# Five expert items of up to 512 tokens in place of eight of up to 256, in a fused attention, expert and SwiGLU kernel

## The chip, the cores and the metric

The kernel runs on one core of one Trainium2 chip. The metric is the device time of one execution in microseconds (us), as the median of three runs. All times of single instructions come from one profiled execution. The engines are named as in the profile: PE (TensorE matmul), PEld (its weight loads), DVE (VectorE), ACT (ScalarE), POOL (GpSimd), SP (SyncE, which here only issues transfers; SPq is its queue).

## The reference

```
# 1. sparse attention: 2 batches, 8 heads, 768 tokens, head size 64; a window of |i-j| < 16 keys
#    and 24 block summaries                                 -> x: 1536 tokens x 512
# 2. experts, one per token (8 of them, 512 -> 1024 -> 512)
logits = x @ w_gate + modality_bias[modality_id]
e_idx = argmax(logits);  gate = softmax(logits)[e_idx]
for e in range(8):
    h = maximum(x[e_idx == e] @ w1[e], 0);  out[e_idx == e] = gate * (h @ w2[e])
# 3. SwiGLU on all tokens (512 -> 1536 -> 512); its weights are float64
g = x @ w_gate2
return (g * sigmoid(g) * (x @ w_val)) @ w_out
```

With the reference's inputs the argmax sends 46 tokens to expert 3, 651 to expert 5 and 839 to expert 6, and none to the other five; of the first 768 tokens 21, 291 and 456.

## The kernel before, in words

Every product of stages 2 and 3 is made in three passes (`mm3`, lines 775 to 778): both operands are split in a high and a low part, and high x high, high x low and low x high are summed in PSUM. The high part is an ACT copy, the low part a subtraction (`split_w`, lines 756 to 763, for weights, on POOL or DVE; `xh`, `xl` for tokens; `hh`, `hl` for the hidden layer, both from PSUM on ACT and DVE).

The stages run one after another on PE: attention (to about 102 us), the items of the experts (to about 302 us), the SwiGLU layer (six slices `fb` of 256 hidden columns by three groups of 512 tokens, 72 matmuls of 512 columns each time).

An **item** is a run of tokens of one expert: a pair (P) is two blocks of 128 tokens, a single (S) one block. `KIND` fixes eight of them, "PPSPPSPP". Item 0 is chosen when the first 768 tokens are routed and runs while the others are; items beyond the eight run in a loop at the end, `For_i(0, n_over)`. For an item POOL gathers the tokens (`xs`, an indirect transfer for each block, line 723), DVE multiplies them by their gate (`scale_x`, line 730), PE turns them (line 740), and then four chunks of the first matrix (`hidden`) and four of the second (`project`) follow. In a pair the weights stand in the array and 256 tokens move: 24 matmuls of 256 columns a chunk, 192 an item. In a single the tokens stand and the weights move: 48 matmuls of 256 columns and 24 of 512.

A chunk is 512 KB of weights. The lists of chunks are loaded and split ahead of use: four buffers for the loaded chunk (`raw`) and four for its parts (`wc`); `split_to(done + 4)` stands ahead of each chunk's products, and a load is issued by SP when a `raw` buffer is free. `POOLS` gives the low part of every second chunk to POOL, the others to DVE.

Routing goes through short DVE operations and small matmuls: `route` (ranks), `route_where`, `route_items(i0, i1)` (a mask `bo` on DVE, line 517, then 24 small matmuls `bo` by `a`, line 523, which give the row numbers `idx` of those items). The program is written out in the order of each engine's queue: an engine that waits holds back all that stands behind it.

The float64 weights of the SwiGLU layer arrive as 64-bit words and are decoded by five DVE operations each (`decode`, lines 1145 to 1167), then split by ACT and POOL. Those of slice 0 are decoded during the last two items, a step behind each chunk (`bg_step`).

Of the kernel before, what the change touches and what calls it, by code (L numbers as in the profile page):

```python
# [19 lines left out]
def sparse_attention_moe_swiglu_kernel(  # L20
# [28 lines left out]
    # queries go in groups of 64; a group sees 96 keys, from 16 before it on, and the summaries of all blocks  # L49
# [20 lines left out]
    NP, NSG = KIND[1:].count("P"), KIND[1:].count("S")  # L70
    MAXP = (NTOK + E * (IT // 2 - 1)) // IT
    NI = 1 + MAXP + E
    NIC = NI * 2
# [20 lines left out]
    b_p = [None, attn.enter_context(tc.tile_pool(name="b1", bufs=1))]  # L94
# [86 lines left out]
    # the mask of the window and the bias of the summaries as a product: ml.T @ mr  # L181
# [16 lines left out]
    # keys: per group of queries the window and the summaries; queries: the two heads of a pair on the diagonal  # L198
# [19 lines left out]
    # the averages over blocks of 32 tokens of a chunk of v, in the rows of the summaries  # L218
# [31 lines left out]
    cs = [const.tile([128, 2, 2 * E], F32, name=f"cs{i}") for i in range(4)]  # L250
# [18 lines left out]
    mtab = const.tile([128, NI, 2, E], F32, name="mtab")  # L269
# [7 lines left out]
    def route_consts():  # L277
# [75 lines left out]
    a1 = {}  # L353

    def route(g, a, b):
# [52 lines left out]
        a0 = w_p.tile([128, 8, 128], BF16, tag="a0", bufs=1, name="a0")[:, 0:n]  # L408
# [12 lines left out]
    def route_early():  # L421
        # the first item: up to 256 tokens of the expert that has the most in the first group
        b = GROUPS[0][1]
        c0 = cnt[:, 0]
        w = w_p.tile([128, 6, E], F32, tag="r_ew", bufs=1, name="r_ew")
# [4 lines left out]
        nc.vector.tensor_scalar(out=n0, in0=m8, scalar1=-1.0, scalar2=float(-IT), op0=ALU.mult, op1=ALU.max)  # L430
        nc.vector.tensor_scalar(out=sc[0][:, 16:17], in0=m8, scalar1=float(IT), scalar2=None, op0=ALU.min)
# [3 lines left out]
        nc.vector.scalar_tensor_tensor(out=w[:, 2, 0:2], in0=fs.to_broadcast([128, 2]), scalar=-16.0, in1=kc[:, 0],  # L435
                                       op0=ALU.mult, op1=ALU.add)
# [3 lines left out]
        TB = [128, b, 2]  # L440
        nc.vector.tensor_tensor(out=bo[:, 0:b, 0:2], in0=w[:, 2, 0:2].unsqueeze(1).to_broadcast(TB),
# [14 lines left out]
        load_to(4)  # L456
# [6 lines left out]
    def route_where():  # L463
        # where the items lie: per expert the pairs and singles before it
# [16 lines left out]
        u = w_p.tile([128, 2, E], F32, tag="r_u", bufs=1, name="r_u")  # L481
        u_r.append(u)
        nc.vector.scalar_tensor_tensor(out=u[:, 1], in0=cs[0][:, 0, E:2 * E], scalar=2.0, in1=wm16, op0=ALU.mult,
                                       op1=ALU.add)
        nc.vector.scalar_tensor_tensor(out=u[:, 0], in0=cs[3][:, 0, E - 1:2 * E - 1], scalar=-2.0, in1=wm16,
                                       op0=ALU.mult, op1=ALU.add)

    def route_items(i0, i1):
        todo = [(gg, a, t) for gg, (a, b) in enumerate(GROUPS) for t in range(b - a)]
        n = i1 - i0  # L490
        IE9 = [128, n, 2, E + 1]
        IE = [128, n, 2, E]
# [9 lines left out]
        mu = w_p.tile(IE, F32, tag=f"r_mu{i0}", bufs=1, name="r_mu")  # L502
        nc.vector.tensor_tensor(out=mu, in0=mtab[:, sl], in1=u_r[0].unsqueeze(1).to_broadcast(IE), op=ALU.mult)
        mu2 = w_p.tile(IE, F32, tag=f"r_mv{i0}", bufs=1, name="r_mv")
# [8 lines left out]
        sl_c = w_p.tile([128, n, 2], F32, tag=f"r_sc{i0}", bufs=1, name="r_sc")  # L513
        nc.vector.tensor_tensor(out=sl_c, in0=kc[:, sl], in1=sm.unsqueeze(2).to_broadcast([128, n, 2]), op=ALU.add)
# [6 lines left out]
        for i, (gg, a, t) in enumerate(todo):  # L521
            for j in range(2):
                nc.tensor.matmul(out=ip[:, 0:2 * n], lhsT=a1[gg, j][:, t, :], rhs=bo[:, a + t, ss],
                                 start=(i == 0 and j == 0), stop=(i == NT - 1 and j == 1))
        nc.vector.tensor_copy(out=idx[:, ss], in_=ip[:, 0:2 * n])
        yield

    def route_starts():
        # first column of each item: the tokens of the items before it
        IE = [128, NI - 1, 2, E]  # L530
# [183 lines left out]
    def open_moe():  # L714
        for nm, n in (("xg", 1), ("h", NC1), ("raw", 4), ("wc", 4)):
            pl[nm] = moe.enter_context(tc.tile_pool(name=nm, bufs=n, side="right", reuse_waits="tile"))
# [649 lines left out]
```

## Time and profile before

| | |
|---|---|
| median of three runs | 616.27 us (615.70 to 616.77) |
| span of the profiled execution, first to last instruction | 614.8 us |
| PE busy | 573.1 us, 93% |
| DVE, ACT, POOL busy | 397.1, 233.4, 197.1 us |
| mean granted clock of TensorE | 0.971 of full speed |

The profiled execution has no other time of its own than its span; the median of the runs is 1.5 us above it. The span is counted from the first instruction to the last. A busy share is an average over stages that have different limits.

### The profile page before, as it was taken

The numbers are of one execution on the slowest core, as the hardware profiler recorded it, in microseconds if no ns is written. First come the engines' busy times: TensorE is split into PE (matmuls) and PEld (weight loads), VectorE is DVE, ScalarE is ACT, GpSimd is POOL, SyncE is SP. The second block draws the span as 40 slices with busy tenths as digits, with TensorE's granted clock in tenths as the row PEclk, the third lists the DMA queues.
The fourth block names the chain that finished last, engine by engine and source line by source line (L and its number), as shares of the span: only waits on it lengthen the run. The fifth ranks groups of instructions, "written<-read, shape, count | busy, mean of one in ns | idle before, by whom it ended". The sixth has DMA issues, their size and how long they took to land.

```text
span 614.8 us, 9915 instructions
## 1 busy us (share of the span) xinstructions
PE 573.1 (93%) x3840; PEld 499.3 (81%) x3840; DVE 397.1 (65%) x616; ACT 233.4 (38%) x375; POOL 197.1 (32%) x222
## 2 busy tenths in 40 slices
PE   6989999779999998977699999999999999999995
PEld 6879988779989997976678888888888888888884
DVE  5577787679987449999116836827835946773332
ACT  5767946425565556454213332211211221221110
POOL 5682013343674556745101211301110310220025
PEclk8979999988999999999899999999999999999998
DMA  9999239463779768662121322402212220200013
GB/s 246 211 224 227 78 88 278 125 209 118 242 261 320 220 223 261 206 206 69 60 81 32 107 69 68 138 0 69 74 63 64 74 68 1 68 1 1 1 68 138
DMA packets 76322, 77.69 MB, mean 126 GB/s; under 512 B 25252, under 2 KB 57008, under 8 KB 76080
## 3 DMA queue, kind: packets, MB, share of 16 engines
q1 hardware_dynamic: 74192, 70.19, 39.7%
q0 software_dynamic: 2080, 6.82, 3.2%
q8 instruction: 32, 0.52, 0.4%
q14 instruction: 18, 0.15, 0.1%
HBM read 70.46 MB, written 6.35 MB: 125 GB/s over the span
## 4 chain that ended last, share of the span: by engine, by line
PE 48%; issue 1%; POOL 1%; POOLq 0%; DVE 0%
PE ps_T L776 11%; PE ps_T L778 11%; PE ps_T L777 11%; PE ps_S L777 3%; PE ps_S L776 3%; PE ps_S L778 3%; PE ps_P L776 1%; PE ps_P L778 1%; PE ps_P L777 1%; PE ps_V L778 1%; PE ps_V L777 1%; PE ps_V L776 1%; POOL out_dram L1313 0%; POOLq L1361 0%; DVE acc L1308 0%
## 5 line engine op out<-in xcount | busy, mean ns | idle before, releaser
L762 POOL TENSOR_TENSOR wl<-da,wh 128x1024 fp32r<-128x1024 f32 x18 | 45.8, 2544 | 228.3 <-ACT wh L761 223.8
L776 PE MATMUL ps_T<-yh,wh 128*128 128x512 f32 x288 | 114.3, 397 | 4.8 <-issue 4.8
L778 PE MATMUL ps_T<-yh,wl 128*128 128x512 f32 x288 | 113.8, 395 | 0.0
L777 PE MATMUL ps_T<-yl,wh 128*128 128x512 f32 x288 | 113.2, 393 | 0.0
L762 POOL TENSOR_TENSOR wl<-raw,wh 128x1024 fp32r<-128x1024 f32 x32 | 82.4, 2577 | 56.8 <-ACT wh L761 55.6
L1291 DVE TENSOR_TENSOR hv<-sg,ps_T 128x512 f32<-128x512 f32 x36 | 24.7, 685 | 95.9 <-PE ps_T L778 95.2
L761 ACT ACTIVATE wh<-raw 128x1024 fp32r<-128x1024 f32 x64 | 67.0, 1056 | 24.1 <-DMA raw<-in_moe_w_dram 14.8
L762 DVE TENSOR_TENSOR wl<-raw,wh 128x1024 fp32r<-128x1024 f32 x32 | 59.0, 1843 | 20.3 <-ACT wh L761 19.9
L776 PEld LDWEIGHTS ps_T<-yh,wh 128*128 128x128 f32 x288 | 54.4, 189 | 17.1 <-issue 5.0
L778 PEld LDWEIGHTS ps_T<-yh,wl 128*128 128x128 f32 x288 | 54.3, 188 | 13.1
L777 PEld LDWEIGHTS ps_T<-yl,wh 128*128 128x128 f32 x288 | 54.5, 189 | 12.7
L1293 ACT ACTIVATE fh<-hv 128x512 fp32r<-128x512 f32 x36 | 22.8, 633 | 110.1 <-DVE hv L1291 110.1
L1289 ACT ACTIVATE sg<-ps_T 128x512 f32<-128x512 f32 x36 | 21.5, 596 | 97.0 <-PE ps_T L778 97.0
L778 PE MATMUL ps_S<-hh,wl 128*128 128x256 f32 x184 | 53.7, 292 | 4.0 <-DVE wl L762 4.0
L777 PE MATMUL ps_T<-xl,wh 128*128 128x256 f32 x192 | 53.9, 281 | 2.7 <-DVE xl L743 2.7
L776 PE MATMUL ps_T<-xh,wh 128*128 128x256 f32 x192 | 54.5, 284 | 0.0
L776 PE MATMUL ps_S<-hh,wh 128*128 128x256 f32 x184 | 54.0, 294 | 0.2 <-DVE ex_r L391 0.2
L777 PE MATMUL ps_S<-hl,wh 128*128 128x256 f32 x184 | 53.4, 290 | 0.4 <-DVE hl L791 0.4
L778 PE MATMUL ps_T<-xh,wl 128*128 128x256 f32 x192 | 53.8, 280 | 0.0
L1295 DVE TENSOR_TENSOR fl<-hv,fh 128x512 fp32r<-128x512 f32 x36 | 25.4, 705 | 25.2 <-ACT fh L1293 25.2
L778 PEld LDWEIGHTS ps_S<-hh,wl 128*128 128x128 f32 x184 | 36.6, 199 | 4.4 <-DVE wl L762 4.4
L777 PEld LDWEIGHTS ps_T<-xl,wh 128*128 128x128 f32 x192 | 36.3, 189 | 3.2 <-DVE xl L743 3.1
(273 smaller groups left out, 1227.4 us busy)
## 6 DMA issues: line engine op xcount, KB each, us to landing
raw<-in_moe_w_dram SPq DMA_DIRECT2D x64, 512.0 KB, 4.0
r<-in_moe_w_gate_dram SPq DMA_DIRECT2D x6, 1024.0 KB, 5.1
r<-in_moe_w_val_dram SPq DMA_DIRECT2D x6, 1024.0 KB, 5.1
r<-in_moe_w_out_dram SPq DMA_DIRECT2D x6, 1024.0 KB, 5.0
ve<-in_v_dram SPq DMA_DIRECT2D x20, 192.0 KB, 5.3
ld<-in_k_dram SPq DMA_DIRECT2D x12, 256.0 KB, 6.0
ld<-in_q_dram SPq DMA_DIRECT2D x12, 256.0 KB, 5.5
x_d<-x SPq DMA_DIRECT2D x12, 256.0 KB, 3.9
```

Of the source, the lines that this page charges most:

```text
L761: nc.scalar.activation(out=wh, in_=src, func=ACTF.Copy)
L762: eng.tensor_tensor(out=wl, in0=src, in1=wh.bitcast(F32), op=ALU.subtract)
L776: nc.tensor.matmul(out=out_, lhsT=ah, rhs=bh, start=start, stop=False)
L777: nc.tensor.matmul(out=out_, lhsT=ah, rhs=bl, start=False, stop=False)
L778: nc.tensor.matmul(out=out_, lhsT=al, rhs=bh, start=False, stop=stop)
L1289: nc.scalar.activation(out=sg, in_=gp_, func=ACTF.Silu)
L1291: nc.vector.tensor_tensor(out=hv, in0=sg, in1=vp_, op=ALU.mult)
L1293: nc.scalar.activation(out=hh, in_=hv, func=ACTF.Copy)
L1295: nc.vector.tensor_tensor(out=hl, in0=hv, in1=hh.bitcast(F32), op=ALU.subtract)
```

## The change

The items are now T (three blocks, 384 tokens), Q (four, 512), S, Q, P: "TQSQP". The pairs' code serves all kinds but S, with the columns of a matmul equal to the item's tokens; where two halves don't fit in one PSUM bank each takes its own. The counts of Q, P and S come from the bits of each expert's count. The second matrix's chunks are now half of the rows by half of the columns (512 x 256 in place of 256 x 512), so that two chunks finish half of the outputs, which are then stored (`store_y`) while the other half is computed; in S the 24 matmuls of 512 columns become 48 of 256. There are three `raw` and three `wc` buffers, four for gathered blocks. POOL makes the low part of every chunk but the odd ones of item 0 and of S (`DVES`). The float64 weights come, and are decoded, in halves of 512 KB; two steps behind each chunk. In item 0 `route_items(2, NI)` comes with its small matmuls between the second and the third chunk of `project`.

```diff
-    KIND = "PPSPPSPP"
+    KIND = "TQSQP"
+    BLOCKS = {"T": 3, "Q": 4, "P": 2, "S": 1}
...
+    RB, WB = 3, 3
     def open_moe():
-        for nm, n in (("xg", 1), ("h", NC1), ("raw", 4), ("wc", 4)):
+        for nm, n in (("xg", 1), ("raw", RB), ("wc", WB)):
...
-            t = pool.tile([128, DM + 1], F32, tag="xs", bufs=2, name="xs")
+            t = pool.tile([128, DM + 1], F32, tag="xs", bufs=4, name="xs")
...
     def load_w(pool, e, which, c):
-            src = w2[bass.ds(e, 1), 256 * c:256 * c + 256, :]
+            src = w2[bass.ds(e, 1), 512 * (c % 2):512 * (c % 2) + 512, 256 * (c // 2):256 * (c // 2) + 256]
...
+    def project(c, hs, w, yp, cols=(0, 1)):
+        for k in range(4):
+            kk = 4 * (c % 2) + k
+            h = hs[kk // 2]
+            for dd in cols:
...
+                mm3(y, w[0][:, k, sl], w[1][:, k, sl], h[0][:, kk % 2, :], h[1][:, kk % 2, :],
...
-    POOLS = [0] + list(range(3, len(preps), 2))
+    DVES = [i for i, (wn, j, c) in enumerate(preps) if (KIND[j] == "S" or i < 2 * NC1) and i % 2]
...
     hidden_0(3)
-    yp = y_banks()
+    yp = [y_banks(CT, "S")]
     project_0(0, False)
...
     xs = gather(pl["xg"], *idx_of(1))
+    rg.append(route_items(2, NI))
     project_0(1)
-    rg.append(route_items(3, NI))
     adv(6)
     scale_x(xs)
-    project_0(2)
-    project_0(3)
-    x = split_of(1, xs)
     while rg:
         adv(1000)
     attn.close()
...
+    store_y(0, yp[0], slice(0, CT), slice(0, CT))
+    yp.append(y_banks(CT, "T"))
+    project_0(2)
+    x = split_of(1, xs)
+    project_0(3)
+    store_y(1, yp[1], slice(0, CT), slice(0, CT))
     sexc = route_starts()
...
         if j == NS - 2:
-            bg += [decode((wn, 0), fw_p) for wn in "gvo"]
+            bg += [decode(wn, 0, i, fw_p) for wn in "gvo" for i in range(2)]
+            load64()
+            load64()
...
         for c in range(NC1):
-            split_to(done + 4)
+            split_to(done + WB)
...
-            bg_step()
+            bg_step(2)
```

**The order on PE** in the second half of item 0, at the small matmuls of the second `route_items`. Before, they stand behind all four chunks of `project` (the rows with `ps_S`) and the turning of item 1's tokens:

```order
L776 MATMUL ps_S<-hh,wh 128x256
L777 MATMUL ps_S<-hl,wh 128x256
L778 MATMUL ps_S<-hh,wl 128x256
L740 MATMUL ps_V<-ident,xs 128x128 x4
L740 MATMUL ps_P<-ident,xs 128x128 x4
L523 LDWEIGHTS a_1421
L523 MATMUL ps_V<-bo,a_1421 128x30
```

Now they stand behind the second chunk, and chunks three and four come after them:

```order
L802 MATMUL ps_S<-hh,wh 128x384
L803 MATMUL ps_S<-hl,wh 128x384
L804 MATMUL ps_S<-hh,wl 128x384
L540 LDWEIGHTS a_1431
L540 MATMUL ps_V<-bo,a_1431 128x76
L540 LDWEIGHTS a_1432
L540 MATMUL ps_V<-bo,a_1432 128x76
```

They have moved ahead of half of `project`, and have 76 columns in place of 30.

**The order on DVE** at the same place: `idx` of item 1, a weight split (`wl`), and the operations of the second `route_items` up to the mask `bo`. Before:

```order
L525 CAST idx<-ps_V 128x4
L762 TENSOR_TENSOR wl<-raw,wh 128x1024
L497 TENSOR_TENSOR r_lt<-cs_203,kk__208 128x270
L500 TENSOR_TENSOR mtab<-r_lt 128x240
...
L517 TENSOR_TENSOR bo<-r_sc,code 128x12x30
L730 TENSOR_SCALAR xs<-xs 128x512 x2
```

Now:

```order
L542 CAST idx<-ps_V 128x4
L789 TENSOR_TENSOR wl<-raw,wh 128x1024
L514 TENSOR_TENSOR r_lt<-cs_203,kk__208 128x513
L517 TENSOR_TENSOR mtab<-r_lt 128x456
...
L534 TENSOR_TENSOR bo<-r_sc,code 128x12x76
L756 TENSOR_SCALAR xs<-xs 128x512 x4
```

The order is the same, each operation is about twice as wide, and four blocks are scaled in place of two.

**The order on POOL** over the last two items, with the gathers (`xs`), the weight splits and the low parts of the decoded weights (`gl`, `vl`, `ol`). Before, from the gather of the last item on:

```order
L723 DMA xs<-x_d,idx 128x513 x2
L762 TENSOR_TENSOR wl<-raw,wh 128x1024 x3
L762 TENSOR_TENSOR wl<-da,wh 128x1024
L762 TENSOR_TENSOR wl<-raw,wh 128x1024
L1183 TENSOR_LOAD tab
L762 TENSOR_TENSOR wl<-raw,wh 128x1024
L762 TENSOR_TENSOR wl<-da,wh 128x1024
```

Now:

```order
L749 DMA xs<-x_d,idx 128x513 x2
L789 TENSOR_TENSOR wl<-raw,wh 128x1024 x3
L1220 TENSOR_TENSOR gl<-da,gh 128x4x128
L789 TENSOR_TENSOR wl<-raw,wh 128x1024 x2
L1220 TENSOR_TENSOR gl<-da,gh 128x4x128
L789 TENSOR_TENSOR wl<-raw,wh 128x1024 x2
L1220 TENSOR_TENSOR vl<-da,vh 128x4x128
```

The low parts of the decoded weights stand between splits that are now all on POOL.

## Rows read from the trace of the kernel before

**Rows 1.** The page: busy time, share of the span and instructions of each engine.

```profile
PE 573.1 (93%) x3840; PEld 499.3 (81%) x3840; DVE 397.1 (65%) x616; ACT 233.4 (38%) x375; POOL 197.1 (32%) x222
```

**Rows 2.** Busy time by stretch: items 0, 2, 4 to 7, the gap behind, SwiGLU.

```profile
core 0: us, PE busy (x) PEld busy (x) DVE busy (x) ACT busy (x) POOL busy (x), PEclk, DMA share, GB/s
102.38:138.56 36.18, 27.29 (x242) 26.23 (x241) 26.66 (x59) 14.26 (x19) 14.44 (x9) 0.91 0.62 179
...
165.03:180.61 15.58, 14.32 (x114) 12.46 (x113) 14.02 (x23) 11.11 (x16) 11.62 (x5) 1.00 0.80 259
...
204.76:228.01 23.25, 23.25 (x198) 23.25 (x197) 10.21 (x12) 11.99 (x16) 11.40 (x6) 1.00 0.73 240
228.01:243.93 15.92, 13.42 (x90) 11.73 (x89) 13.93 (x17) 11.01 (x16) 10.35 (x6) 1.00 0.89 281
243.93:270.03 26.10, 24.59 (x205) 24.19 (x204) 24.23 (x19) 13.62 (x18) 16.78 (x8) 1.00 0.63 205
270.03:301.83 31.80, 25.11 (x194) 24.10 (x192) 24.41 (x21) 10.90 (x15) 14.10 (x6) 0.95 0.23 70
301.83:306.60 4.77, 0.00 (x1) 0.01 (x1) 0.42 (x1) 1.67 (x2) 0.00 (x0) 0.96 0.42 120
306.60:604.80 298.20, 298.20 (x1285) 242.26 (x1286) 168.85 (x205) 65.08 (x99) 47.47 (x31) 0.99 0.17 57
```

**Rows 3.** What PE waited for, longest in total first.

```profile
PE ps_V L523 <- DVE bo L517: 5.3, 1, 5.3
PE ps_T L776 <- issue: 4.8, 1, 4.8
PE ps_V L740 <- DVE xs L730: 4.4, 2, 3.0
PE ps_S L778 <- DVE wl L762: 4.0, 2, 2.1
PE ps_T L777 <- DVE xl L743: 2.7, 2, 2.3
```

**Rows 4.** Busy time by stretch, inside runs of matmuls of one width.

```profile
125.16:128.51 3.35, 3.35 (x21) 3.35 (x19) 1.71 (x3) 0.00 (x0) 1.06 (x2) 0.50 0.60 187
204.76:216.07 11.31, 11.31 (x99) 11.31 (x97) 5.73 (x7) 6.27 (x9) 5.24 (x3) 1.00 0.85 278
330.84:347.50 16.66, 16.66 (x73) 13.48 (x73) 15.02 (x14) 6.49 (x10) 4.98 (x2) 1.00 0.40 127
```

**Rows 5.** Groups of instructions: count, busy us, mean ns, idle before.

```profile
L762 POOL TENSOR_TENSOR wl<-raw,wh 128x1024 fp32r<-128x1024 f32 x32 | 82.4, 2577 | 56.8 <-ACT wh L761 55.6 <-DVE wl L762 1.1
L761 ACT ACTIVATE wh<-raw 128x1024 fp32r<-128x1024 f32 x64 | 67.0, 1056 | 24.1 <-DMA raw<-in_moe_w_dram 14.8 <-PE ps_S L777 7.0 <-POOL wl L762 1.3
L762 DVE TENSOR_TENSOR wl<-raw,wh 128x1024 fp32r<-128x1024 f32 x32 | 59.0, 1843 | 20.3 <-ACT wh L761 19.9
L723 POOL DMA_INDIRECT xs<-x_d,idx x14 | 17.4, 1242 | 18.3 <-PE ps_P L740 6.6 <-DVE code L453 4.6 <-DVE idx L525 4.5
```

**Rows 6.** Timeline of DVE: start us, duration us.

```profile
209.37 1.23 DVE L762 TENSOR_TENSOR wl<-raw,wh 128x1024 fp32r<-128x1024 f32 x1 [0.26 <-ACT wh L761]
...
248.80 2.85 DVE L1152 TENSOR_SCALAR da<-r 128x1024 int32<-128x1024 int32 x1
...
252.29 3.44 DVE L762 TENSOR_TENSOR wl<-raw,wh 128x1024 fp32r<-128x1024 f32 x1
```

**Rows 7.** Timeline of POOL at the same places.

```profile
248.67 2.42 POOL L762 TENSOR_TENSOR wl<-raw,wh 128x1024 fp32r<-128x1024 f32 x1
251.86 2.79 POOL L762 TENSOR_TENSOR wl<-raw,wh 128x1024 fp32r<-128x1024 f32 x1 [0.77 <-ACT wh L761]
```

**Rows 8.** Timeline of DVE: first and last of nine operations of `route_items`.

```profile
135.19 0.43 DVE L497 TENSOR_TENSOR r_lt<-cs,kk__208 128x270 f32<-128x270 f32 x1
...
137.58 0.53 DVE L517 TENSOR_TENSOR bo<-r_sc,code 128x360 bf16<-128x360 f32 x1
```

**Rows 9.** The 64 loads of expert weights: from issue to landing.

```profile
DMA to landing us min/median/max: 3.2/4.0/8.8
```

**Rows 10.** Timeline of ACT: the high part of a decoded weight, and its wait.

```profile
293.39 1.06 ACT L761 ACTIVATE wh<-da 128x1024 fp32r<-128x1024 f32 x1 [7.95 <-DVE da L1162]
```

More of the change, by code (lines that the diff above doesn't have):

```diff
@@ L66, in sparse_attention_moe_swiglu_kernel @@
     IT = 256
-    KIND = "PPSPPSPP"
+    KIND = "TQSQP"
+    BLOCKS = {"T": 3, "Q": 4, "P": 2, "S": 1}
     NS = len(KIND)
[L70 to L73, printed above, removed]
+    NQ, NP, NSG = (KIND.count(kd) for kd in "QPS")
+    CT = 128 * BLOCKS["T"]
+    MAXQ = 3
+    assert 385 * (MAXQ + 1) > NTOK and NQ <= MAXQ
+    NOQ, NOP = 2 * (MAXQ - NQ), E - NP
+    NI = NS + NOQ + NOP + E - NSG
+    NB = 4
+    NIC = NI * NB
     KD = DM // 128
@@ new lines, in hidden, with low @@
+        for f0 in range(0, 2, per):
+            p = bank("T")[:, 0:per * n].rearrange("p (f c) -> p f c", f=per)
+            for f in range(f0, f0 + per):
+                sl = slice(128 * f, 128 * f + 128)
+                for kk in range(KD):
+                    mm3(p[:, f - f0, :], w[0][:, kk, sl], w[1][:, kk, sl], x[0][:, kk, :], x[1][:, kk, :], kk == 0,
+                        kk == KD - 1)
+            fs = slice(f0, f0 + per)
+            nc.scalar.activation(out=hh[:, fs], in_=p, func=ACTF.Relu)
+            def low(p=p, fs=fs):
+                nc.vector.scalar_tensor_tensor(out=hl[:, fs], in0=p, scalar=0.0, in1=hh[:, fs].bitcast(F32),
+                                               op0=ALU.max, op1=ALU.subtract)
+            if later is None:
+                low()
+            else:
+                later.append(low)
@@ new lines, in y_banks, with store_y @@
+    def y_banks(n, tag):
+        if n == 256:
+            return [bank(tag).rearrange("p (d c) -> p d c", d=2)]
+        return [bank(tag)[:, 0:n].rearrange("p (d c) -> p d c", d=1) for _ in range(2)]
+    def store_y(dp, yp, a, v_):
+        for i, y in enumerate(yp):
+            nd = 2 // len(yp)
+            ds = slice(2 * dp + nd * i, 2 * dp + nd * i + nd)
+            nc.scalar.activation(out=yh[:, ds, a], in_=y, func=ACTF.Copy)
+            nc.vector.tensor_tensor(out=yl[:, ds, v_], in0=y, in1=yh[:, ds, v_].bitcast(F32), op=ALU.subtract)
@@ L1038, in project_0 @@
         if split:
-            split_to(NC1 + c + 4, 2 * NC1 if c == 0 else None)
-        project(c, hs[c], ready.pop(("w2", 0, c)), yp)
+            split_to(NC1 + c + WB, 2 * NC1 if c == 0 else None)
+        project(c, hs, ready.pop(("w2", 0, c)), yp[c // 2])
     hs, later = [], []
@@ L1053, in sparse_attention_moe_swiglu_kernel @@
         adv(1000)
[L1054 removed]
+    rg.append(route_items(1, 2))
     adv(6)
@@ L1163, in decode @@
                                        op1=ALU.bitwise_or)
-        if key[0] == "g":
-            load64("o", key[1])
+        load64()
         yield
-        fw[key] = split_w(pool, a.bitcast(F32), nc.gpsimd, (key[0] + "h", key[0] + "l"))
+        if i == 0:
+            whole = [128, 2, DM] if wn == "o" else [128, KD, 256]
+            fw[wn, fb] = [pool.tile(whole, F32R, tag=wn + x, name=wn + x) for x in "hl"]
+        part = (slice(None), slice(i, i + 1)) if wn == "o" else (slice(None), slice(None), slice(128 * i, 128 * i + 128))
+        wh, wl = (t[part] for t in fw[wn, fb])
+        nc.scalar.activation(out=wh, in_=a.bitcast(F32), func=ACTF.Copy)
+        nc.gpsimd.tensor_tensor(out=wl, in0=a.bitcast(F32), in1=wh.bitcast(F32), op=ALU.subtract)
     def bg_step(n=1):
@@ L1175, in bg_step, with before @@
                 bg.pop(0)
-    store_y(yp, slice(0, IT), slice(0, IT))
+    store_y(0, yp[0], slice(0, CT), slice(0, CT))
[4 more added lines that the diff above has]
+    store_y(1, yp[1], slice(0, CT), slice(0, CT))
     sexc = route_starts()
+    def before(j):
+        return min(NTOK, sum(128 * BLOCKS[kd] for kd in KIND[:j]))
     done = 2 * NC1
```

386 lines of the change are left out of this document (195 added, 191 removed).

## The prediction

> **What bounds the kernel now.** I read the page's busy table first: PE works 93% of the span [rows 1], so only what PE does, or waits for, can change the time. The stretches come next, cut at the items [rows 2]. In SwiGLU PE is busy for 298.20 of 298.20 us; nothing in the change makes its 1296 matmuls fewer, so no gain is to be had there. From the first product of item 0 to the last of item 7 it is 102.38 to 301.83, 199.45 us, and the items differ: item 4, a pair, takes 23.25 us with PE busy throughout, but item 0 takes 36.18 with PE busy for 27.29, item 6 takes 26.10 and item 7 takes 31.80 with 25.11 busy; the singles, 15.58 and 15.92. The chain of waits says for what [rows 3]: in item 0 the mask `bo` (5.3 us) and the scaled tokens (3.0 us of the 4.4), late in the last items `wl` and `xl`, all of them on DVE, which is busy 24.23 of 26.10 and 24.41 of 31.80 us there [rows 2]. A wait costs more than itself: behind the 5.3 us the granted clock is 0.50, the level of 1.2 GHz, for 3.35 us [rows 4], half of which is lost.
>
> DVE is that slow because of POOL. One `wl` takes 1.23 us on DVE alone; at 252.29 it took 3.44, and its end lies 1.08 us behind the end of the POOL split that began at 251.86 for 2.79; the decoding step at 248.80 likewise ends 0.56 us behind POOL's [rows 6, 7]. So one of the two waits for the other, instruction by instruction.
> The page "SBUF — State Buffer" of the Trainium skill, section "SBUF: two separate sides", says the same: a DVE operation of two SBUF inputs, or in a two-port mode, and a GpSimd operation lock a shared port pair for the whole instruction. The trace agrees (3.44 against 1.23 us); if they shared it by halves instead, the S item below would cost some 4 us less.
>
> **The change part by part.**
>
> *Matmuls.* The columns stay 1792 (384+512+128+512+256 against six times 256 and two times 128), but wide matmuls are cheaper by the column: 96 of 256 columns take 11.31 us, 117.8 ns each, and 72 of 512 take 16.66, 231.4 ns [rows 4] (the counts in the rows hold the neighbours still in flight). So a Q saves 192 x (2 x 117.8 - 231.4) = 0.8 us against two pairs; T's 384 columns, which no row shows, lie between the two, 175 ns by the middle. By themselves the wider matmuls give some 2 us. The gain must come from the waits.
>
> *The stages one by one*, against item 4's 23.25 us = 192 x 117.8 ns + 0.6 for four transposes and the like.
>
> T: 192 x 0.175 = 33.5. Routing's small matmuls take about 1.7 (item 0's 27.29 busy, less 22.6 for its pair, less some 3 at half clock); 16 transposes of item 1's tokens 1.5 (at most 0.16 each by item 4's rest, 0.09 taken); 76 columns in place of 30, 0.6. The first mask keeps its place on PE, behind the first chunk of `project`, but each chunk ahead of it lasts 4.2 us rather than 2.8, so it should be ready: 5.3 us gone. In its place comes a **new wait**: the small matmuls of the second `route_items` stand between chunks two and three of `project`, and PE holds for its mask. Nine DVE operations took 135.19 to 138.11, 2.9 us [rows 8]; twice as wide, about 5. They begin behind a `wl` that can't start before chunk one ends (its buffer) and takes ACT 1.06 and DVE 1.23, so 2.3 + 5 = 7.3 us against chunk two's 4.2: 3.1 us late, 3.5 taken; nothing at best, 8 if the lock adds two POOL splits. Behind PE stand chunks three and four and item 1. The same wait again costs 1.5 at half clock. A third gathered block ahead of item 0: at most a further 1.24 [rows 5], 0.9 taken; and 0.8 for `project`'s waits on its weights, since on POOL the split of chunk three stands behind four gathers of 1.24. T: 44.
>
> Q: 192 x 0.2314 = 44.4, with 4 to 8 transposes and stores 0.8, and 0.8 for item 1's first bank, freed behind `route_starts` on DVE: 46.0 each. A chunk lasts 5.6 us, so one load of 4.0 (8.8 at worst [rows 9]), one ACT copy of 1.06 and one POOL split of 2.58 [rows 5] are covered by two chunks in hand. The decoding hides here too: two half steps a chunk, about 0.6 us each and up to 2.4 of waiting for POOL, beside two `hl` of 0.7: 5.2 to 7.4 a chunk at the worst, 3.5 as a rule.
>
> S: 96 x 117.8 ns = 11.3, with 16 transposes 1.5, token matmuls and turns 1.4: 14.2 of work. The buffers hold two chunks ready; the other six need three splits on POOL (2.58) and three on DVE (1.23), one after another: 11.4 us, and the scaling of four blocks (1.7) on the same port. With 1.06 for ACT and as much for its two stores ahead, and 1.4 for the last chunk, 16.7; the ring of three `raw` buffers can't refill faster than (4.0 + 1.06 + 2.58) / 3 = 2.5 a chunk, which adds 2 to 4. I take 20.3; 15.5 at best (the singles' 1.3 us of waiting as now), 26 at landings of 8.8: (8.8 + 3.6) / 3 = 4.15 for six chunks.
>
> P, the last: 22.6 + 0.6, and 1.0 for a late split: POOL makes all eight (20.6 of 22.6 us). No DVE split is left in it, where the last two pairs had eight: that is where 6.69 us of item 7's wait go. 24.2; bounds 23.25 and 31.8.
> The page "GPSIMD Engine Reference", section "Key points", puts DVE at about twice GpSimd's speed for elementwise work, which speaks against this move; 1.23 against 2.58 us agrees, and the decoding rival below is priced by it.
>
> *At nothing:* the gap of 4.77 us behind the items stays. The 24 chunks of 512 KB that are no longer loaded only free the queues. Half-size decoding in SwiGLU gives DVE 15 more short operations a slice; by their widths [rows 8] (0.10 us for 90 more elements, so 0.13 fixed) that is 2 us a slice, on 168.85 busy of 298.20. PE's 49.7 us a slice cover it; without that cover it would be 10 us in five slices.
>
> Sum: T 44 + 2 x 46.0 + 20.3 + 24.2 = 180.5 against 199.45, **-19**; I keep 0.5 for DVE operations I haven't listed: -18.4. The span becomes 596.4, and with the 1.5 us by which the median stands above it, **598 us**.
>
> **The rivals.**
>
> 1. *As summed*, 593 to 603. Chance 0.53.
> 2. *The new waits don't come*: the mask ready in time (T 39.5), S with its present waits (16.5), P clean: 10 less, 588. For it: the DVE chain at 135.19 ran without a split of POOL beside it. Against: DVE is the busier engine in every row where PE waits [rows 2]. 0.15.
> 3. *The lock hits the new order harder*: two POOL splits inside the mask's chain (+4.8, and half clock), S at 26, P at 28: 607 to 612. For it 3.44 against 1.23. 0.20.
> 4. *Slower: decoding holds POOL.* POOL's queue has six low parts of decoded weights between splits that are now all its own, and each stands behind ACT, which waited 7.95 us for DVE's decoding [rows 10]. Half the size, half the wait: 4 us, six times 24: 598 + 24 = 622. It decides from 3.1 us each (18.4 / 6). Against: a Q chunk has 3 us of slack, and DVE has lost 24 of its 32 splits (1.84 each, 44 us). 0.05.
> 5. *The change doesn't do what it says*: an item is left over and runs in the loop. By the inputs' counts T takes 384 of expert 6, which leaves 455 (one Q), 651 (a Q and a P) and 46 (an S): exactly the list. 640 or fewer in place of 651 would leave one over, for at least 22.6 + a load and split of 7.6 + gathers, 36: 634. 0.02.
> 6. *No change that can be told*: rivals 3 and 4 in part. 0.05.
>
> **How the numbers follow.** The likeliest is 598. 588 to 610 takes in rivals 1 to 3 but for their ends, about 0.82. A change within 0.2% (1.2 us) is about what a measurement of this kernel can't tell from none. Faster by more: 0.53 + 0.15 + 0.20 and a little of 6, 0.90; same 0.03; slower 0.07.
>
> **What would show it.** PE's stretches: T 42 to 46 us with one wait of 3 to 5 us for `bo` before the 76-column matmuls, clock 0.50 behind it; each Q 45 to 47 with PE busy all through; S 18 to 23 with waits for `wl` and `hl`; P under 25; SwiGLU 298 again. No ACT wait for `da` above 4 us. DVE busy at most two thirds of each Q. It is wrong if a Q shows waits on `wh` or `wl` (loading or POOL bounds after all), if P passes 28 (rival 4), if the loop runs, or if SwiGLU is no longer full.

## The result and the profile after

The changed kernel took 621.29 us (median of 13 runs, 618.17 to 624.77) against 618.19 for the kernel before (13 runs, 615.70 to 620.59): ratio 1.0065, 95% interval 1.0041 to 1.0090. The forecast was 598 (588 to 610); it was wrong in its sign too. The profiled execution has a span of 622.1 us and took 623.85, above its median, so its stretches sum to more than the 3.1 us between the medians.

The page's busy row of the changed kernel, as [rows 1]:

```profile
PE 575.0 (92%) x3396; PEld 486.2 (78%) x3396; DVE 381.9 (61%) x688; ACT 212.3 (34%) x370; POOL 194.5 (31%) x252
```

PE's stretches in the changed kernel, columns as in [rows 2]: T, Q, S, Q, P, the gap, SwiGLU.

```profile
109.11:163.06 53.95, 44.69 (x283) 43.28 (x281) 31.13 (x72) 17.36 (x29) 17.59 (x11) 0.85 0.32 100
163.06:207.70 44.64, 44.64 (x197) 36.43 (x197) 21.47 (x47) 15.53 (x22) 23.87 (x13) 1.00 0.34 114
207.70:231.55 23.85, 18.69 (x145) 17.17 (x144) 15.71 (x22) 12.45 (x18) 9.31 (x5) 0.86 0.53 173
231.55:278.10 46.55, 45.77 (x207) 37.21 (x205) 28.19 (x33) 18.13 (x26) 29.49 (x15) 1.00 0.54 174
278.10:308.58 30.48, 25.41 (x193) 24.59 (x191) 22.48 (x20) 11.33 (x17) 18.95 (x9) 0.94 0.35 116
308.58:313.98 5.40, 0.00 (x1) 0.01 (x1) 0.43 (x1) 1.67 (x2) 0.00 (x0) 0.95 0.03 6
313.98:612.18 298.20, 298.20 (x1286) 242.22 (x1287) 185.24 (x280) 67.50 (x114) 48.33 (x46) 1.00 0.17 56
```

Both Qs are full, the second but for a wait of 0.78 us for a `wl`, and as long as forecast (91.2 us, 92.0 said), and SwiGLU is the same 298.20 us. The loss lies in the three others. From 102.38, where item 0 began before, T takes 60.7 us, not 44: its first product comes at 109.11, and then it takes 53.95. S takes 23.85, not 20.3, and P 30.48, not 24.2. These are 16.7 + 3.6 + 6.3 = 26.6 us more than forecast.

What PE waited for in the changed kernel (reader, releaser and line: us in total, times, longest), as [rows 3]:

```profile
PE ps_V L540 <- DVE bo L534: 4.6, 1, 4.6
PE ps_S L804 <- POOL wl L789: 4.5, 2, 2.4
PE ps_V L717 <- DMA ve<-ve: 4.3, 2, 4.2
PE ps_T L802 <- DVE hl L822: 3.5, 1, 3.5
PE ps_S L804 <- DVE hl L871: 3.2, 2, 2.1
PE ps_V L768 <- DVE xs L756: 2.6, 1, 2.6
PE ps_P L768 <- DVE xl L771: 2.2, 3, 1.1
```

The wait for `bo` was forecast (3.5). The ones for `hl` (L822) and `xs` lie in T and were not. The wait for `ve` lies in the attention, at 37.7, and comes and goes from execution to execution: in the traces of the changed kernel and of its ten variants below, which don't alter that part, the first transposes of tokens behind the attention began between 98.8 and 102.3 us. The 1.7 us by which they began later here than before (102.34 against 100.64) is therefore not put down to the change.

Three times in T a DVE operation ended with a POOL split that had begun within 0.2 us of it. First DVE, then POOL in the changed kernel's timeline (start us, duration us):

```profile
102.87 2.49 DVE L756 TENSOR_SCALAR xs<-xs 128x512 f32<-128x512 f32 x1 [0.76 <-DMA xs<-x_d,idx]
125.49 2.24 DVE L492 TENSOR_TENSOR cs<-cs 128x24 f32<-128x24 f32 x1
145.09 2.47 DVE L531 TENSOR_TENSOR r_sc<-kc,r_sm 128x76 f32<-128x76 f32 x1
```

```profile
102.75 2.34 POOL L789 TENSOR_TENSOR wl<-raw,wh 128x1024 fp32r<-128x1024 f32 x1 [5.95 <-DMA raw<-in_moe_w_dram]
125.31 2.38 POOL L789 TENSOR_TENSOR wl<-raw,wh 128x1024 fp32r<-128x1024 f32 x1 [0.24 <-ACT wh L788]
145.10 2.35 POOL L789 TENSOR_TENSOR wl<-raw,wh 128x1024 fp32r<-128x1024 f32 x1
```

Elsewhere in these traces they take 0.48, 0.18 and 0.22 us. Each stands on the way to one of PE's waits: `xs` at 105.42, the chain of the first mask ahead of the deferred `hl` at 130.06, the second mask `bo` at 148.75. On DVE the first mask and the deferred `hl` came in this order:

```profile
129.33 0.21 DVE L534 TENSOR_TENSOR bo<-r_sc,code 128x48 bf16<-128x48 f32 x1
129.46 1.01 DVE L822 SCALAR_TENSOR_TENSOR hl<-ps_T,hh 128x384 fp32r<-128x384 f32 x2
```

and on PE the wait for that `hl` came ahead of the products that use the mask:

```profile
130.06 0.69 PE L802 MATMUL ps_T<-xh,wh 128*128 128x384 f32 x1 [3.53 <-DVE hl L822]
139.10 0.76 PE L540 MATMUL ps_V<-bo,a 128*128 128x4 bf16 x24
```

The waits cost twice: right behind the 3.5 us for `hl`, PE works 4.01 us at a granted clock of 0.50, which is 1.2 GHz.

```profile
130.06:134.07 4.01, 4.01 (x13) 4.01 (x13) 2.01 (x3) 0.00 (x0) 0.00 (x0) 0.50 0.41 136
```

In P the last chunk's copy on ACT stands behind a decoded weight's, as in rival 4. Two of the forecast's own signs of being wrong came with it: P past 28 us, and a wait of ACT for `da` above 4 us. ACT's timeline, with the wait in brackets, then POOL's split of the same chunk and PE's wait for it:

```profile
299.88 0.63 ACT L1219 ACTIVATE oh<-da 128x512 fp32r<-128x512 f32 x1 [5.36 <-DVE da L1210]
300.42 1.04 ACT L788 ACTIVATE wh<-raw 128x1024 fp32r<-128x1024 f32 x1
```

```profile
301.85 2.35 POOL L789 TENSOR_TENSOR wl<-raw,wh 128x1024 fp32r<-128x1024 f32 x1
```

```profile
304.25 0.39 PE L804 MATMUL ps_S<-hh,wl 128*128 128x256 f32 x1 [2.08 <-POOL wl L789]
```

So there were two theories. One: a handful of separate waits, each made by the order of a queue (DVE's, ACT's, SP's) and by the lock between DVE and POOL, make the loss, and each can be mended. The rival: the splits, most of them now on POOL, bound the items, so that a wait taken away comes back.

### The profile page after: what moved, and what is told of

Read it like the earlier page. It is cut to its first block, busy times and chain, and to the rows that moved or that the text cites. A ratio compares the mean times of both kernels' runs of the same rounds, so it can differ in the third digit from the quotient of the medians.

```text
span 622.1 us, 9023 instructions
## 1 busy us (share of the span) xinstructions
PE 575.0 (92%) x3396; PEld 486.2 (78%) x3396; DVE 381.9 (61%) x688; ACT 212.3 (34%) x370; POOL 194.5 (31%) x252
## 4 chain that ended last, share of the span: by engine, by line
PE 48%; issue 1%; POOL 1%; POOLq 0%; DVE 0%
PE ps_T L802 11%; PE ps_T L804 11%; PE ps_T L803 11%; PE ps_S L803 3%; PE ps_S L802 3%; PE ps_S L804 3%; PE ps_V L804 1%; PE ps_P L802 1%; PE ps_V L803 1%; PE ps_V L802 1%; PE ps_P L803 1%; PE ps_P L804 1%; POOL out_dram L1381 1%; POOLq L1426 0%; POOL tk L1380 0%
## 5 line engine op out<-in xcount | busy, mean ns | idle before, releaser
L802 PE MATMUL ps_T<-yh,gh 128*128 128x512 f32 x144 | 57.5, 399 | 5.4 <-issue 5.4
L804 PE MATMUL ps_T<-yh,gl 128*128 128x512 f32 x144 | 57.1, 396 | 0.0
L803 PE MATMUL ps_T<-yl,gh 128*128 128x512 f32 x144 | 56.9, 395 | 0.0
L802 PE MATMUL ps_T<-yh,vh 128*128 128x512 f32 x144 | 56.8, 394 | 0.0
L804 PE MATMUL ps_T<-yh,vl 128*128 128x512 f32 x144 | 56.7, 394 | 0.0
L803 PE MATMUL ps_T<-yl,vh 128*128 128x512 f32 x144 | 56.3, 391 | 0.0
L802 PE MATMUL ps_T<-xh,wh 128*128 128x512 f32 (+2 forms) x128 | 47.0, 367 | 3.5 <-DVE hl L822 3.5
L804 PE MATMUL ps_T<-xh,wl 128*128 128x512 f32 (+2 forms) x128 | 46.6, 364 | 1.4 <-POOL wl L789 1.4
L803 PE MATMUL ps_T<-xl,wh 128*128 128x512 f32 (+2 forms) x128 | 46.4, 363 | 0.0
L822 DVE SCALAR_TENSOR_TENSOR hl<-ps_T,hh 128x512 fp32r<-128x512 f32 (+1 forms) x28 | 17.8, 648 | 26.9 <-ACT hh L819 26.9
L1207 DVE SCALAR_TENSOR_TENSOR db<-r,da 128x512 int32<-128x512 int32 x36 | 31.9, 887 | 0.2
```

The costliest lines, as they stand in the source:

```text
L802: nc.tensor.matmul(out=out_, lhsT=ah, rhs=bh, start=start, stop=False)
L803: nc.tensor.matmul(out=out_, lhsT=ah, rhs=bl, start=False, stop=False)
L804: nc.tensor.matmul(out=out_, lhsT=al, rhs=bh, start=False, stop=stop)
L822: nc.vector.scalar_tensor_tensor(out=hl[:, fs], in0=p, scalar=0.0, in1=hh[:, fs].bitcast(F32), op0=ALU.max, op1=ALU.subtract)
L1207: nc.vector.scalar_tensor_tensor(out=b, in0=lo, scalar=29, in1=a, op0=ALU.logical_shift_right, op1=ALU.bitwise_or)
```

## The experiments

No kernel here leaves any of the computation out. Ratios are to the kernel before, run on the same chip beside each; the changed kernel's is 1.0065. The intervals are 0.4 to 0.8% wide, 2 to 5 us. The ratios aren't those of the two medians; by the medians, each less that of the kernel before beside it, the gains named below come out up to 2.7 us smaller (5.1 us for e1_hl_now, 1.7 for e6_dec_q2, 10.0 for e7_all). Only e1_hl_now, e6_dec_q2, e7_all, e9_mend2 and e10_mend_rb4 have intervals that lie apart from the changed kernel's.

**`hl` at once** (e1_hl_now).

```diff
-    hidden_0(2, later)
+    hidden_0(2)
```

> The changed kernel, with the low parts `hl` of the first item's third hidden chunk made at once on DVE, not behind the mask's chain. Theory A (single waits in the first item make the loss): a T chunk now needs two banks, so the fourth hidden chunk waits for those `hl`; PE's wait of 3.5 us at 130.06 goes, and with it about 2.0 us of half clock behind it (4.01 us at 0.50); the mask's chain then starts 1.0 us later and still ends before the first chunk of `project` does. 5.5 us faster than the changed kernel: 616, ratio to the kernel before about 0.997. Rival B (the splits on POOL bound the item, so a wait that is taken away comes back at the next `wl`): the wait appears at `wl` or `bo` in the next 20 us, the stretch 109 to 163 keeps its 54.0 us within 1.5, 620.

Ratio 0.9970 (0.9946 to 0.9994), 615.54 us: 5.9 us from the changed kernel (the difference of the ratios, 0.0095, times 618; so below). The wait is gone, and T's 53.95 us are 46.81:

```profile
106.56:153.37 46.81, 41.08 (x283) 39.95 (x282) 28.90 (x72) 17.41 (x29) 17.61 (x11) 0.93 0.37 115
```

The waits for `bo` (4.6) and `xs` (2.6) stayed as they were. This one deferred operation is more than the whole loss against the kernel before: with it mended, the changed kernel is the faster one, if by little.

**Small matmuls later** (e2_small_behind).

```diff
     adv(6)
     scale_x(xs)
+    yp.append(y_banks(CT, "T"))
+    project_0(2)
     while rg:
         adv(1000)
```

> The changed kernel, with the small matmuls of the second `route_items` behind the third chunk of the first item's `project` in place of ahead of it. Theory A: PE's 4.59 us wait for `bo` and 1.5 to 2 us of half clock go (one chunk of 4.27 at full clock covers them): T 6 us shorter, 615. Rival B: the third chunk meets its own weights late (their split on POOL began at 145.10 behind four gathers and ended at 147.45), so 3 of the 6 us come back as a wait for `wl`: 618. Rival C (a later list of tokens makes the gathers of the third item late): under 1 us, since they are only issued in the second item.

Ratio 1.0034 (1.0009 to 1.0059), 619.53 us: 1.9 us. The wait for `bo` went, and this came at 143.14, as rival B had it:

```profile
143.14 0.44 PE L804 MATMUL ps_T<-hh,wl 128*128 128x384 f32 x1 [3.00 <-POOL wl L789]
```

**First split on DVE** (e3_dve0).

```diff
-    split_to(1, 2 * NC1)
     scale_x(first_x[0])
+    split_to(1, 2 * NC1)
```

with chunk 0 added to `DVES`.

> The changed kernel, with the first weight split on DVE, behind the scaling of the first item's tokens, in place of POOL. Theory A (the lock): the third scaled block took 2.49 us beside POOL's split of 102.75 to 105.09, where 0.48 is its own time; alone it ends at 103.4, the split takes DVE 1.23 behind it: the first hidden matmul comes 2 us earlier (107.1), total 619. Rival B: the block is late because its gather lands late, and the split on DVE (1.23) stands before the four `xl`, so no more than 0.5 us changes: 621.

Ratio 1.0045 (1.0021 to 1.0069), 619.94 us: 1.2 us, within the interval of either. PE's longest wait for `xs` fell from 2.6 to 0.8 us, a wait of 1.3 for `z`, which now stands behind the split on DVE, came in its place, and from the first transposes to the first product it was 4.9 us (6.8 in the changed kernel). e2_small_behind, with the order of the changed kernel, had 4.3. There the last scaling began 0.11 us ahead of POOL's split, and in the changed kernel 0.12 us behind it (102.87 and 102.75): 0.49 us against 2.49. DVE and POOL in e2_small_behind:

```profile
101.41 0.49 DVE L756 TENSOR_SCALAR xs<-xs 128x512 f32<-128x512 f32 x1 [0.53 <-DMA xs<-x_d,idx]
```

```profile
101.52 2.59 POOL L789 TENSOR_TENSOR wl<-raw,wh 128x1024 fp32r<-128x1024 f32 x1 [6.02 <-PE ps_V L768]
```

A lead of 0.11 us was enough there; leads of 0.01 us (`r_sc` at 145.09 above) and 0.02 us (`r_sc` in e2_small_behind, 4.81 us) were not. In the other six traces with that order PE's longest wait for the `xs` of item 0 was 2.2 to 2.7 us, so e2_small_behind was the lucky one. What this mend gives depends on which of the two comes first in an execution.

**Decoding in the Qs only** (e4_dec_q).

```diff
-        if j == NS - 2:
+        if j == 1:
             bg += [decode(wn, 0, i, fw_p) for wn in "gvo" for i in range(2)]
...
-            bg_step(2)
+            if kd == "Q":
+                bg_step(2)
```

> The changed kernel, with the decoding of the first slice in the two items of 512 tokens alone, from the second item on, and none in the items of 128 and 256. Theory A (the decoding's copies `gh`, `vh`, `oh` hold ACT's queue in the last item, and the weight copies stand behind them): the waits for `wl` of 2.41 and 2.08 us in the last item go, P from 30.5 to 25 us, total 616, each Q within 1 us of before (44.6 and 46.55). Rival B (POOL alone can't make the eight splits of P in time, at 2.5 us each against 2.9 us of PE a chunk, or the loads bound it): P stays above 28, 620. Rival C: the decoding moves its wait into the second item, which has routing work on DVE: Q1 grows by more than 3 us, and the total stays.

Ratio 1.0032 (1.0007 to 1.0058), 619.36 us: 2.0 us. Q, S, Q, P of this kernel:

```profile
159.62:204.27 44.65, 44.65 (x198) 36.43 (x197) 38.81 (x61) 17.21 (x25) 27.09 (x16) 1.00 0.53 171
204.27:232.80 28.53, 19.96 (x145) 18.21 (x144) 18.61 (x29) 12.52 (x18) 10.57 (x5) 0.82 0.52 166
232.80:279.30 46.50, 45.72 (x206) 37.24 (x205) 24.57 (x25) 18.00 (x26) 29.46 (x15) 1.00 0.43 140
279.30:302.49 23.19, 23.19 (x193) 22.98 (x191) 5.26 (x8) 10.13 (x14) 14.41 (x6) 1.00 0.25 85
```

P is 23.19 us and full, with all its splits on POOL: the decoding was what held it, not POOL. S gave 4.7 of the 7.3 us back. DVE had the rows of the sorted order and the decoding in the second half of the first Q (38.81 us busy, 21.47 in the changed kernel) and came late into S, which waits for its outputs (`yl` 1.7 us) and `h` (1.0). The longest wait in S is another, for `hh`:

```profile
218.38 0.58 PE L802 MATMUL ps_S<-wh,hh 128*128 128x256 f32 x1 [3.24 <-ACT hh L870]
```

This `hh` stood on ACT behind a weight copy that had waited 3.80 us for its load, and SP issued its next load for the experts only at 211.04, behind one of the decoding's at 210.44. So both DVE's lateness and the late loads point to the decoding. Rival C named the place, though the waits fell behind the item it had named.

**Small matmuls later, and the split ahead of them on DVE** (e5_small_split6): e2's edit, with chunk 6 in `DVES` in place of 7.

> The changed kernel with the small matmuls of the second `route_items` behind the third chunk of `project` as in e2_small_behind, and the split of that third chunk on DVE (idle from 135.4 there), the one of the fourth on POOL. Theory A (in e2 the wait for `bo` of 4.6 us came back as 3.0 us for a `wl` that stood behind four gathers on POOL): PE has no wait over 1.5 us between the first chunk of `project` and the second item, T is 6 to 7 us shorter than in the changed kernel, total 615, ratio 0.996. Rival B (splits are too slow as such): a wait of 2 us or more for the `wl` of the fourth chunk, or for `xl`, total 618.

Ratio 1.0061 (1.0028 to 1.0093), 620.91 us: nothing that the medians can tell. The wait for `wl` went, and another came behind it. PE, DVE and POOL:

```profile
146.60 1.27 PE L768 MATMUL ps_V<-ident,xs 128*128 128x128 f32 x3 [2.52 <-DVE xs L756]
```

```profile
140.65 6.69 DVE L756 TENSOR_SCALAR xs<-xs 128x512 f32<-128x512 f32 x4
```

```profile
141.56 4.70 POOL L789 TENSOR_TENSOR wl<-raw,wh 128x1024 fp32r<-128x1024 f32 x2
```

Four scalings that take 1.67 us for the four in the changed kernel took 6.69 beside two POOL splits. This mend met the rival theory in its mild form: the wait came back twice, each time at another place of DVE's or POOL's queue, this time at one that neither expectation had named. (T itself was 50.28 us in this one profile; the medians don't show these 3.7 us.)

**Decoding away from the rows of the sorted order** (e6_dec_q2): e4's edit, but no step in the second half of the first Q.

> The changed kernel with the first slice's decoding in the hidden half of the second item (8 steps) and in the fourth item (16 steps), none elsewhere. Theory A (e4's gain of 7 us in P was given back in S, since decoding in the second half of Q1 made DVE late for the rows of the sorted order and the S item's first low parts): P 23 to 24 us, S 23 to 25 in place of 28.5, Q's unchanged, total 614.5, ratio 0.994. Rival B (S is late for its loads: in e4 its fifth weight copy waited 3.8 us for DMA behind the six decoding loads): S stays at 27 or more, 618.

Ratio 1.0001 (0.9973 to 1.0029), 618.00 us: 4.0 us. S is 24.27, as expected, but P 26.48: it still waits twice for `wl` (2.8 together). Since this edit took the decoding's steps and its loads out of the second half of the first Q together, it doesn't tell which of the two had held S. Here the decoding ended only in P, and SP issued the first of P's last three loads at 284.60, 6.2 us into P and behind the decoding's load at 283.36; ACT's copy of that chunk began at 291.05. In e4_dec_q the same load went out 4.5 us into P (283.77), with none of the decoding's beside it. That SP's order makes this wait is argued from these times; that it goes when the decoding ends sooner is shown by e9_mend2. The second of the two waits also stands behind a decoded weight's low part on POOL, of 1.29 us.

**All mends** (e7_all).

> All the mends at once: `hl` of the third hidden chunk at once, the small matmuls and splits of e5_small_split6, the first split on DVE behind the scaling, the decoding of e6_dec_q2. Theory A (each wait stands by itself): -6.0 (e1), -6 (e5), -1.5 (e3), -7 (e6) from the changed kernel's 621: about 601, ratio to the kernel before 0.973 (0.97 to 0.978). Rival B (the waits lie behind one another on the same splits, so that one mended lays open the next): half of it, 611, ratio 0.989.

Ratio 0.9860 (0.9820 to 0.9900), 609.67 us: 12.7 us, about the sum of what its parts gave alone (5.9 + 0.2 + 1.2 + 4.0), and far from the sum of the waits that they removed: rival B's size, not theory A's 601. Left were 1.8 us for `xs` beside two POOL splits, with a slow clock behind them, and 3.3 for `wl` in P.

**Further moves** (e9_mend2): e7_all with

```diff
-    DVES = [i for i, (wn, j, c) in enumerate(preps) if (KIND[j] == "S" and i % 2) or i in (0, 1, 3, 5, 6)]
+    DVES = [i for i, (wn, j, c) in enumerate(preps) if (KIND[j] == "S" and i % 2) or i in (0, 1, 3, 5, 6, 7, 8)]
...
-            if c == NC1 - 1 and not last:
+            if c == NC1 - 1 and not last and kd != "S":
                 scale_x(xs)
...
                     hs += [turn_h1(h) for h in h1[2:]]
+                    scale_x(xs)
```

and three decoding steps a chunk in the second Q, so that it ends there.

> e7_all with three further moves: the splits of the first item's fourth second-matrix chunk and of the next item's first chunk on DVE, so that no POOL split lies beside the scaling of the second item's tokens; the S item's scaling behind its low parts; the decoding at three steps a chunk in the fourth item, over before the last item. Theory A (the lock of DVE's scaling by POOL's splits, and SP's loads behind the decoding's, are what is left): T 4 us shorter (no wait of 1.8 us for `xs`, no half clock behind it), S 1 to 2 shorter, P 23.2 in place of 27.3: 9 us from e7_all's, 601, ratio 0.973 to 0.977. Rival B (DVE becomes the bound with the further splits and steps): waits for `wl` or `bo` on DVE appear in T or for `hl` in the fourth item, half the gain or less, 606 and more.

Ratio 0.9767 (0.9740 to 0.9794), 601.37 us, as theory A had it. T, Q, S, Q, P:

```profile
106.03:148.21 42.18, 39.41 (x282) 37.73 (x281) 28.80 (x74) 17.59 (x29) 14.52 (x9) 0.99 0.41 137
148.21:192.86 44.65, 44.65 (x198) 36.46 (x197) 34.94 (x57) 16.07 (x23) 25.63 (x14) 1.00 0.51 160
192.86:214.62 21.76, 17.89 (x145) 16.60 (x144) 13.68 (x22) 12.33 (x18) 8.86 (x5) 0.92 0.63 192
214.62:261.12 46.50, 45.72 (x206) 37.28 (x205) 29.39 (x35) 19.16 (x28) 31.88 (x17) 1.00 0.51 160
261.12:284.32 23.20, 23.20 (x193) 22.98 (x191) 5.26 (x8) 10.02 (x14) 14.42 (x6) 1.00 0.27 89
```

T has no wait above 1.5 us and a clock of 0.99. The decoding lies in the Qs (DVE busy 34.94 and 29.39 us) and costs them nothing.

**A fourth load buffer** (e8_rb4): the changed kernel with

```diff
-    RB, WB = 3, 3
+    RB, WB = 4, 3
```

the decoding in place, without its tile `db`, and one small tile of the routing shared, to make room.

> The changed kernel with four buffers for loaded weights in place of three, in S's room: the decoding works in place without its second buffer. Theory A (S is bound by the ring of three loads, as its ACT copies that waited 1.1 to 3.8 us for DMA say): S 20 to 21 in place of 23.9, with T and P some 1 us shorter, total 616, ratio 0.998. Rival B (S is bound by the token scaling on DVE beside a POOL split, 3.4 us ahead of the low parts `hl`, and by ACT's order): S within 1 us of 23.9, total 620 to 621. Rival C: the in-place decoding or more loads in flight cost something elsewhere: over 622.

Ratio 1.0053 (1.0035 to 1.0071), 619.86 us: 0.7 us, too little to tell. The trace says more: S is 21.52 us, not 23.85. Its waits for `hh` are down to 0.25 us, those for `hl` are 0.7 and 2.1, the longer one behind four scalings of 3.77 us. So the ring of loads held S. The scaling did too: in e9_mend2, where it stands behind the low parts, the wait of 2.1 is gone.

**Both** (e10_mend_rb4): e9_mend2 with e8_rb4's edits.

> e9_mend2 with the four load buffers and the in-place decoding of e8_rb4. Theory A (with the scaling out of the way, S is left with its copies on ACT that wait for loads, 1.1 us for `hh` and 1.15 for `hl` in e9_mend2; the fourth buffer took the same waits from e8_rb4): S 19.5 to 20.5 in place of 21.8, total 599.5, ratio 0.973. Rival B (the loads are no longer last in S): S within 0.7 of 21.8, total 601.4 as e9_mend2.

Ratio 0.9721 (0.9686 to 0.9756), 601.06 us, the best of all; its interval overlaps e9_mend2's. S is 19.13 us at full clock:

```profile
196.26:215.39 19.13, 16.52 (x145) 15.03 (x144) 13.65 (x22) 12.22 (x18) 9.54 (x5) 1.00 0.67 214
```

**One part alone: half-size decoding in the kernel before** (b1_half_dec). Its edit is the change's own in `load64`, `decode` and the steps, at the old places.

> The kernel before with one part of the change alone: half-size decoding, two steps in place of one at each place, its items as they were. Theory A (half the size makes ACT's wait for the decoding shorter, but the last pairs are still bounded by it): items 6 and 7 some 2 us shorter together, SwiGLU the same, 616, ratio 0.997. Rival B (15 more short DVE operations and six more copies a slice cost DVE in the last pairs more than they give): 2 to 4 us slower, ratio 1.004.

Ratio 1.0038 (1.0008 to 1.0068), 620.05 us. Rival B: this part alone costs some 2 us. The last two pairs took 61.3 us (57.9 before).

**The same mend in the kernel before** (b2_dec_mid): b1_half_dec with the decoding in items 3 and 4.

> The kernel before with half-size decoding in its items 3 and 4, two steps a chunk, and none in its last two. Theory A (the decoding held the last pairs of the kernel before just as it holds the changed one's last item): items 6 and 7 from 57.9 to 49 us, items 3 and 4 one or two longer, total 609, ratio 0.987. Rival B (the last pairs wait for splits and loads by themselves, four DVE splits each of 1.23 to 3.4 us): items 6 and 7 stay above 54, total 614 to 616.

Ratio 1.0062 (1.0039 to 1.0086), 620.24 us. Items 3, 4, 6 and 7:

```profile
180.32:209.74 29.42, 26.00 (x205) 25.40 (x204) 21.22 (x27) 12.55 (x18) 16.35 (x9) 0.94 0.76 244
209.74:242.13 32.39, 25.78 (x198) 24.95 (x197) 29.21 (x31) 15.20 (x21) 19.01 (x11) 0.95 0.65 215
...
259.63:283.77 24.14, 24.14 (x205) 24.13 (x204) 16.94 (x14) 12.89 (x17) 14.05 (x7) 1.00 0.64 206
283.77:306.76 22.99, 22.99 (x194) 22.79 (x192) 7.72 (x10) 8.90 (x13) 7.21 (x3) 1.00 0.19 67
```

Half of the expectation held: the last pairs are now full, with their DVE splits as they were. But the two pairs with the decoding have taken over their waits, 61.8 us in place of the 24.15 and 23.25 that items 3 and 4 take in b1_half_dec and, item 4, before [rows 2]. At the two places that were tried the pairs have no room for it; the Qs of e9_mend2 have. This is a part of what the change is worth, and what its first form didn't use. Not tried is the kernel before with its own waits in item 0 mended (5.3 us for `bo`, 3.0 for `xs`): how much of the gain of e9_mend2 it would get with its narrow items is open.

## Why the prediction was wrong

*Right in size:* the Qs, SwiGLU, and the gap (5.40, 4.77 said). DVE's extra work in SwiGLU was 16.4 us, not 10, and hidden. By columns, too: 72 matmuls of 512 took 16.82 us in a full stretch of e9_mend2, and the first Q is 1.9 us shorter than two of item 4 (the second, 46.55, is as long as two).

*T, the step that failed.* "The first mask keeps its place on PE ... so it should be ready: 5.3 us gone" was true of the mask, which DVE had made at 129.5, long before PE came to it at 139.1. But the step looked only at who waits for the mask, not at what stands behind its chain on DVE: the deferred `hl` of the third hidden chunk. With 256 columns a chunk takes one of the three T banks; with 384 its two halves take one each, so the second half of the fourth chunk needs the bank that this `hl` has still to read. The page "PSUM — Partial Sum Buffer" of the Trainium skill, section "The four PSUM rules", says that a matmul's output lies in one bank of 512 fp32 columns; 2 x 384 are more. The traces agree in that the wait is there with 384 columns and was not with 256, where DVE made the same `hl` while PE was long past the fourth hidden chunk (DVE, then PE, in the kernel before):

```profile
124.39 0.68 DVE L791 SCALAR_TENSOR_TENSOR hl<-ps_T,hh 128x512 fp32r<-128x512 f32 x1
```

```profile
115.70 0.28 PE L776 MATMUL ps_S<-hh,wh 128*128 128x256 f32 x1
```

In none of my rivals did this wait occur. It cost 5.9 us by e1_hl_now; in the trace it is about 6.1 of T's 16.7 us too many, 3.5 of waiting and some 2.6 for 18 matmuls that follow 0.32 us apart in place of 0.175. The second step, the new wait for `bo`, was foreseen and somewhat larger (4.6 against 3.5, and its clock). The third, the late start with 0.9 us, was 5.0 (6.7 less the attention's 1.7): I counted the third gather, and not the first POOL split that its scaling would meet (2.49 us in place of 0.48). That is about half of it: in e2_small_behind, where the scaling wasn't held, the first product still came 4.3 us behind the first transposes, against 1.7 before.

*P.* "No DVE split is left in it" took away the wrong wait: in b2_dec_mid the last pairs keep their DVE splits and are full as soon as the decoding is elsewhere. The splits on POOL alone do keep up (e4_dec_q), as the sum said; the copies of the decoding on ACT don't let them. That is rival 4's mechanism, which I priced at six waits of 4 us and gave 0.05. It came with two that mattered (3.99 and 5.36 on ACT) and cost 6.3 us in P.

*S.* The ring, the "2 to 4 us" of the step, was there (2.3 by e8_rb4). The scaling of four blocks I had counted at 1.7; beside a POOL split the four took 3.77, ahead of `hl`. Term 20.3, measured 23.85.

*The rivals.* Rival 3, the lock with 607 to 612, had the right mechanism in T and S, and rival 4 had P's. In T the three held operations ran 6.3 us over their own time (2.0, 2.1 and 2.25), and the last two are parts of the waits for `hl` and for the second `bo`. With both rivals, and with a wait that I hadn't seen, nothing was left of the gain of 18.4 us. (Rival 2's own terms come to 9.3 less, 4.5 + 3.8 + 1.0, not 10.) With the waits mended most of it is there: in e9_mend2 T takes 42.2 from its first product, which comes 6.6 us behind the first transposes of tokens, against 1.7 before, so 47.1 counted as the sum counts it; then Q 44.7 and 46.5, S 21.8, P 23.2. That is 183.2 us against the 180.5 of the sum, in a kernel of 601 us. The sum priced the kernel as it could be ordered. The order that was written has waits in three items, which I had priced at 3.5 + 1.5 us in T, 2 to 4 in S and 1.0 in P. What stays open is why single mends of DVE's order (e2, e5) gave so little in the medians while their traces show T 3.7 us shorter. A part of it is that a trace is one execution: in e4, e6 and e8, where T's order is the changed kernel's, T took 52.9, 53.9 and 51.6 us, and the 13 runs of the changed kernel go from 618.17 us at a mean granted clock of 0.977 to 624.77 at 0.962, with the profiled one (0.960) among the longest.

## What to carry to other kernels

When a tile gets wider, count the banks or buffers that each step holds, and for each deferred reader ask which next writer needs its bank. Price a queue by what stands behind the late instruction, on every engine that it passes (a decoded copy on ACT, a load on SP), and not only by who reads its result. A mend tried alone can show little since the wait moves on: alone they gave 0.2 to 5.9 us, four of them together 12.7, and with the further moves, which followed the waits to their next places and weren't run alone, 18 to 21.

## What the runs showed of the hardware

An operation of 24 elements a partition takes as long as the POOL split beside it (2.24 us for 0.18). DVE operations that read PSUM weren't held so: of the 14 that began inside a POOL split, single rows between 95 and 320 us of the changed kernel's trace, none ran over its usual time. In P, DVE's `hl`, with one operand in PSUM, ran in its usual time inside a POOL split, and the next, with both in SBUF, waited for the split's end. DVE, then POOL:

```profile
287.86 0.68 DVE L822 SCALAR_TENSOR_TENSOR hl<-ps_T,hh 128x512 fp32r<-128x512 f32 x1
288.46 2.29 DVE L1207 SCALAR_TENSOR_TENSOR db<-r,da 128x512 int32<-128x512 int32 x1
```

```profile
287.62 2.60 POOL L789 TENSOR_TENSOR wl<-raw,wh 128x1024 fp32r<-128x1024 f32 x1
```

The page "SBUF — State Buffer" of the Trainium skill, section "SBUF: two separate sides", names the DVE operations that lock the shared ports: those in a two-port mode and those with two SBUF inputs. The rows agree for `cs`, `r_sc` and `db`, with two inputs in SBUF, which were held, and for `hl`, with one, which wasn't. By the page the scaling, with one input and 0.48 to 2.49 us, must then be in a two-port mode, which no row names. Not all work from SBUF is held: in the kernel before a reciprocal took its usual 0.18 us at 101.15, inside a POOL split of 101.05 to 103.41. So work on DVE that reads PSUM can stand beside POOL's splits; the scalings and the operations of two SBUF inputs are what to keep away from them.
